# Attention and feed-forward on one core: the first two batches share seven products on half of w_in's columns, attention runs in two TensorE visits per pair, and the first pair is normalised ahead of the branch

**Chip, cores, metric.** One core of one Trainium2 chip. The metric is device microseconds of a whole execution; lower is better. The kernel before takes 1549 us, and its executions agree within 0.5%.

## The reference

```python
batch, n_heads, seq, head_dim = (8, 12, 448, 64)
n_tokens, d_model, d_ff = (3584, 768, 2048)

def rmsnorm(x, g):
    return x / np.sqrt(np.mean(x * x, axis=-1, keepdims=True) + 1e-06) * g
q_n, k_n = rmsnorm(q, g_q), rmsnorm(k, g_k)
scores = q_n @ k_n.transpose(0, 1, 3, 2) / np.sqrt(64)
attn = np.exp(scores - np.max(scores, axis=-1, keepdims=True))
attn = attn / (np.sum(attn, axis=-1, keepdims=True) + 1e-09)
x = heads_joined(attn @ v)                 # 3584 x 768
h = x @ w_in
out = (h * (1.0 / (1.0 + np.exp(-h)))) @ w_out
```

The arithmetic is fp32. The work is 48 pairs of heads (n = 0 to 47, six to a batch), then a second layer that only multiplies. The weights arrive in 64-bit words: ScalarE *opens* a piece of them, then VectorE and GpSimd *round* it to fp32.

## The kernel before

Both feed-forward layers use seven products of quarter matrices in place of eight (Strassen-Winograd); `sum_x` and `sum_w_in` form, on VectorE, the sums of quarters that these need. `seven` builds each product in one of two PSUM banks named mm, in the order 1 2 6 5 7 3 4; ScalarE empties products 1 and 5, VectorE the others. Each emptying is called its *eviction* here.

```python
def bank(n):
    return ps.tile([P, BANK], F32, name="mm", bufs=2)[:, 0:n]
...
    def product(name):
        t = bank(n)
        for i, s in enumerate(steps):
            nc.tensor.matmul(t, left(name, s), right(name, s), start=i == 0, ...)
            yield n
        return t
    nc.scalar.copy(p1, (yield from product("1")))
    plus((yield from product("2")), p1, done[1, 1])        # plus: a VectorE add
    plus((yield from product("6")), p1, u2)
    nc.scalar.copy(p5, (yield from product("5")))
    plus((yield from product("7")), u2, u3)
    ...                                                    # two adds on GpSimd
    plus((yield from product("3")), u2, done[1, 2])
    plus((yield from product("4")), u3, done[2, 1])
```

This is a generator. The loop over the pairs calls `fill()` to put some of its matmuls (*filler*) between parts of the attention. If a filler ends with a product's last matmul, that product's eviction is issued only when the next filler resumes the generator.

```python
def divide(n):
    t = ps.tile([P, S], F32, name="tr")      # one bank, also used by transpose()
    for h in range(2):
        nc.tensor.matmul(t[...], ones[0:R, :], es[:, h, :], start=True, stop=True)
    nc.vector.reciprocal(out=r, in_=t)
    nc.vector.tensor_tensor(out=xT(*pairs[n]), in0=xU, in1=r, op=ALU.mult)
...
for n, (b, hp) in enumerate(pairs):
    load(n + 2)
    scores(0);              fill()           # half of the scores
    if n > 0: divide(n - 1)                  # sums of e (ones), reciprocal, multiply
    ...
    weigh(n, 0); scores(1); add_up(0)
    ...                                      # batch 1: round w_in
    fill()
    transpose(n + 1, "q")
    weigh(n, 1); unload(n); add_up(1)
    ...
    fill()
    transpose(n + 1, "k"); normalise(n + 2)
    ...
    fill()
```

Batch 0 has no filler. In batches 1 to 3 the filler is `whole(0)`, batch 0's first layer by plain products (96 matmuls of 448 columns), then batch 1 alone by seven products of 224 columns. The pairs n = 24 to 35 carry the seven products of batches 2 and 3, and so on.

## Time and profile before

| | before |
|---|---|
| median of 4 runs | 1549.01 us (1548.05 to 1550.51) |
| span of the profiled run | 1543.8 us |
| mean granted TensorE clock | 0.991 |

### The profile page before, as it was taken

Reading aid. Unit: us, or ns where it says so; the run is one execution under the profiler, and the core shown is the slowest. Engines: PE = TensorE matmul, PEld = TensorE weight load, DVE = VectorE, ACT = ScalarE, POOL = GpSimd, SP = SyncE. Lnnn points to the kernel's source line nnn. Section 1 sums busy time; section 2 is a strip of 40 time slices with the busy share of each in tenths; the row PEclk is TensorE's granted clock in tenths of the full one; section 3 lists DMA queues with packets and bytes.
Section 4 is the critical chain, followed back from the end, with each engine's and each line's share of the span. In section 5 each row is a group of like instructions: output and inputs, shape, how many; then the busy total and the mean of one; then the engine's idle time right before and its main releaser. Section 6 shows DMA issues by size and latency. Waiting matters only on the chain. (4 is left out here: it accounts for less than half of the span.)

```text
span 1543.8 us, 14413 instructions
## 1 busy us (share of the span) xinstructions
PE 1464.2 (95%) x5216; PEld 743.5 (48%) x5216; DVE 759.0 (49%) x970; ACT 525.3 (34%) x744; POOL 408.7 (26%) x300
## 2 busy tenths in 40 slices
PE   5789999899899999999999989999999999999998
PEld 2234444555444444344444344445555555555554
DVE  4988876655765555665555575662121112121221
ACT  4558865555544544544444423420000000000000
POOL 4555533333333323332333223330000000000000
PEclk9999999999899999999999999999999999999999
DMA  6344221121211211311131064442222222222220
GB/s 194 96 128 144 72 78 55 60 61 60 72 60 48 85 59 42 103 60 60 42 102 42 27 212 131 155 149 76 75 75 75 75 75 75 75 75 86 75 85 23
DMA packets 87924, 128.96 MB, mean 84 GB/s; under 512 B 5924, under 2 KB 70948, under 8 KB 87844
## 3 DMA queue, kind: packets, MB, share of 16 engines
q1 hardware_dynamic: 87520, 127.95, 26.5%
q8 instruction: 43, 0.70, 0.2%
q14 instruction: 37, 0.30, 0.1%
q10 hardware_dynamic: 324, 0.00, 0.0%
HBM read 87.56 MB, written 40.37 MB: 83 GB/s over the span
## 5 line engine op out<-in xcount | busy, mean ns | idle before, releaser
L434 PE MATMUL mm<-x,W 128*128 128x448 f32 (+1 forms) x768 | 283.4, 507 | 14.7 <-DVE stage L408 13.1
L335 POOL TENSOR_TENSOR rms<-rms,minus_half 112x16 f32<-112x16 f32 x48 | 141.0, 2937 | 408.4 <-DVE rms L332 394.9
L368 ACT ACTIVATE work<-sc 112x896 f32<-112x896 f32 x192 | 166.1, 914 | 203.3 <-PE sc L365 203.0
L434 PE MATMUL mm<-sums_x,W 128*128 128x448 f32 (+1 forms) x576 | 210.9, 500 | 14.7 <-DVE parts L408 9.3
L434 PEld LDWEIGHTS mm<-x,W 128*128 128x128 f32 x768 | 141.1, 192 | 148.6 <-issue 122.8
L446 POOL TENSOR_TENSOR parts<-parts 128x448 f32<-128x448 f32 (+2 forms) x46 | 49.2, 1069 | 582.1 <-DVE parts L408 581.8
L434 PE MATMUL mm<-W,work 128*128 128x384 f32 x588 | 197.6, 486 | 0.0
L365 PE MATMUL sc<-work 64*112 64x448 f32 x768 | 175.4, 577 | 17.8 <-DVE work L358 17.8
L399 DVE RECIPROCAL work<-tr 128x448 f32<-128x448 f32 x48 | 141.8, 2953 | 88.7 <-PE tr L398 88.7
L408 DVE TENSOR_TENSOR stage<-mm,parts 128x448 f32<-128x448 f32 (+2 forms) x121 | 67.7, 562 | 237.5 <-PE mm L434 101.2
L408 DVE TENSOR_TENSOR parts<-mm,parts 128x448 f32<-128x448 f32 (+2 forms) x92 | 51.6, 561 | 265.7 <-PE mm L434 256.5
L388 DVE TENSOR_TENSOR work<-work 112x896 f32<-112x896 f32 x144 | 169.0, 1174 | 12.1 <-ACT work L368 5.5
L377 PE MATMUL av<-work,rows 112*64 112x448 f32 x768 | 165.3, 552 | 3.6 <-ACT work L368 3.6
L434 PEld LDWEIGHTS mm<-sums_x,W 128*128 128x128 f32 x576 | 104.5, 190 | 105.6 <-issue 79.5
L434 PEld LDWEIGHTS mm<-W,work 128*128 128x128 f32 x588 | 111.7, 190 | 77.9
L365 PEld LDWEIGHTS sc<-work 64*112 64x112 f32 x768 | 62.4, 176 | 115.7 <-issue 63.8
L441 ACT COPY parts<-mm 128x448 f32<-128x448 f32 (+2 forms) x46 | 21.8, 474 | 268.9 <-PE mm L434 268.9
L434 PE MATMUL mm<-W,x 128*128 128x384 f32 x336 | 112.9, 486 | 0.0
L340 POOL TENSOR_TENSOR work<-rows,rms 112x512 f32<-112x512 f32 x96 | 100.6, 1069 | 3.8
L444 ACT COPY parts<-mm 128x448 f32<-128x448 f32 (+2 forms) x46 | 22.1, 481 | 221.9 <-PE mm L434 221.9
L377 PEld LDWEIGHTS av<-work,rows 112*64 112x64 f32 x768 | 50.6, 138 | 82.3 <-issue 53.5
L434 PEld LDWEIGHTS mm<-W,x 128*128 128x128 f32 x336 | 63.8, 190 | 44.5
(66 smaller groups left out, 1437.4 us busy)
## 6 DMA issues: line engine op xcount, KB each, us to landing
hidden<-stage SPq DMA_DIRECT2D x48, 448.0 KB, 2.5
work<-hidden SPq DMA_DIRECT2D x7, 2048.0 KB, 9.0
x<-hidden SPq DMA_DIRECT2D x7, 2048.0 KB, 9.0
W<-in_moe_w_in_dram SPq DMA_DIRECT2D x24, 512.0 KB, 4.1
rows<-in_moe_w_out_dram SPq DMA_DIRECT2D x32, 384.0 KB, 3.1
rows<-in_q_dram SPq DMA_DIRECT2D x48, 224.0 KB, 3.6
rows<-in_k_dram SPq DMA_DIRECT2D x48, 224.0 KB, 3.8
rows<-in_v_dram SPq DMA_DIRECT2D x48, 224.0 KB, 3.6
```

Source lines behind the costliest of these rows:

```text
L335: nc.gpsimd.tensor_tensor(out=flat, in0=flat, in1=minus_half[0:R].to_broadcast([R, 4 * J]), op=ALU.pow)
L340: nc.gpsimd.tensor_tensor(out=normal[name].rearrange("p j h d -> p h j d"), in0=st[name], in1=factor.to_broadcast([R, 2, J, D]), op=ALU.mult,)
L365: nc.tensor.matmul(banks[:, h, 0:S], kT[rows, ts(j, R)], qT[rows, :], start=True, stop=True)
L368: nc.scalar.activation(e[j], banks[:, :, 0:S], AF.Exp)
L377: nc.tensor.matmul(st["av"][ds(h * D, D), :], st["v"][:, h, j, :], e[j][:, h, :], start=(j == 0), stop=(j == J - 1),)
L388: nc.vector.tensor_tensor(out=es, in0=e[0] if j == 1 else es, in1=e[j], op=ALU.add)
L399: nc.vector.reciprocal(out=r, in_=t)
L408: nc.vector.tensor_tensor(out=out, in0=a, in1=b, op=ALU.add)
L434: nc.tensor.matmul(t, left(name, s), right(name, s), start=i == 0, stop=i == len(steps) - 1)
L441: nc.scalar.copy(p1, (yield from product("1")))
L444: nc.scalar.copy(p5, (yield from product("5")))
L446: nc.gpsimd.tensor_tensor(out=u2, in0=u2, in1=p5, op=ALU.add)
```

## The change

The intent: no more 224-column products (batches 0 and 1 take plain products for the first half of w_in's columns and share seven full-width products for the second), one change of TensorE's form fewer per pair, and an earlier start. Cut to its core:

```diff
-        if name == "q":
-            nc.scalar.copy(features[name], t)
+        dst = features[name][n % 2]                    # qT and kT are doubled
+        if name == "q":
+            nc.scalar.copy(dst, t)
+        elif n < 2 * z.NPAIR:
+            nc.scalar.activation(dst, t, AF.Copy, scale=gains)
         else:
-            nc.vector.tensor_scalar_mul(out=features[name], in0=t, scalar1=gains)
+            nc.vector.tensor_scalar_mul(out=dst, in0=t, scalar1=gains)
...
     def first_two():
-        yield from whole(0)
+        yield from whole(1, early)                     # first 8 of 16 column blocks
         for c in range(HW):
-            sum_x([1], c)
-        yield from halves_in([1])
+            sum_x([0, 1], c)
+        yield from halves_in([0, 1], late)
...
+    def weights_in(n, point):                          # when w_in is rounded
+        if n < NPAIR:
+            count = point == 3
+        else:
+            count = n < 5 * NPAIR // 2 and (point % 2 or n < NPAIR + 3 and point == 0)
+        ...
-    for n, (b, hp) in enumerate(pairs):
-        (the loop shown above)
+    for n in range(last + 2):
+        b, hp = pairs[n] if n <= last else (z.B, 0)
+        if n <= last:
+            scores(n, 0)
+        if n > 0:
+            weigh(n - 1, 1)
+            unload(n - 1)
+            divide(n - 1)
+        load(n + 2)
+        ...                                            # begin a group of filler
+        weights_in(n, 0)
+        fill()
+        weights_in(n, 1)
+        transpose(n + 1, "q")
+        scores(n, 1)
+        weigh(n, 0)
+        add_up(0)
+        transpose(n + 1, "k")
+        add_up(1)
+        weights_in(n, 2)
+        ...                                            # at a group's end: finish(), sum_x
+        fill()
+        weights_in(n, 3)
+        normalise(n + 2)
```

Besides, `normalise` of pair 0 stands ahead of the branch (by the size of the gains the program picks one of two versions of itself), with VectorE in place of GpSimd for its multiply; the last two stores are halved; and the scratch for raw weights is smaller for the later half of w_in.

## The prediction

> **What bounds the kernel now.** I read the page first, then the groups by form, the chain of waits in order of time, and TensorE's timeline. n counts the 48 pairs of heads (six per batch), so n = 6 opens batch 1 and n = 24 batch 4.
>
> ```profile
> PE 1464.2 (95%) x5216; PEld 743.5 (48%) x5216; DVE 759.0 (49%) x970; ACT 525.3 (34%) x744; POOL 408.7 (26%) x300
> ...
> PE   5789999899899999999999989999999999999998
> ```
>
> TensorE is the bound in all but the first 100 us. A faster helper engine buys nothing; only TensorE's columns, its changes of form and its idle time count.
>
> ```profile
> L434 PE MATMUL mm<-sums_x,W 128*128 128x448 f32 x432 | 178.5, 548 | 13.0 <-DVE parts L408 9.3 <-ACT parts L441 2.8 <-DVE stage L408 0.9
> ...
> L388 DVE TENSOR_TENSOR work<-work 112x896 f32<-112x896 f32 x144 | 169.0, 1174 | 12.1 <-ACT work L368 5.5
> ...
> L399 DVE RECIPROCAL work<-tr 128x448 f32<-128x448 f32 x48 | 141.8, 2953 | 88.7 <-PE tr L398 88.7
> ...
> L434 PE MATMUL mm<-x,W 128*128 128x224 f32 x192 | 46.9, 376 | 13.9 <-DVE stage L408 12.3 <-ACT stage L472 1.6
> ```
>
> The last line is the weak spot that the change aims at: batch 1 alone runs its seven products on 224 columns, and these wait for VectorE to empty the two PSUM banks.
>
> ```profile
> 790.92 3.02 PE mm L434 x8
> 793.95 1.69 PE sc L365 x8
> 795.64 2.45 PE mm L434 x6
> 798.09 0.90 PE tr L398 x4
> 798.99 1.50 PE av L377 x8
> 800.50 1.69 PE sc L365 x8
> 802.19 3.20 PE mm L434 x8
> ```
>
> In this chain a matmul is two records. Eight mm records after transposes take 3.02 us, so a matmul of 448 columns takes 0.755; after scores the same eight take 3.20. One pair of steady state (n = 25 to 34) starts every 20.1 us with 15 such matmuls (11.3), so the pair's own attention work and changes of form cost 8.75.
>
> **What the Trainium skill says.** "TensorEngine Tiling (Array Packing)", Key Properties: changing the tiling mode drains TensorE. The trace agrees and prices it: 0.18 us (3.20 against 3.02). "TensorE: Matmul & The Clock Gate", section on the 16 sub-arrays: VectorE and ScalarE work strictly in order. The trace agrees:
>
> ```profile
> 519.91 2.96 DVE L399 RECIPROCAL work<-tr 128x448 f32<-128x448 f32 x1 [6.39 <-PE tr L398]
> 521.30 1.76 PE L365 MATMUL sc<-work 64*112 64x448 f32 x8
> ...
> 522.90 0.62 DVE L400 TENSOR_TENSOR x<-work 128x448 f32<-128x448 f32 x1
> 522.99 3.27 PE L434 MATMUL mm<-x,W 128*128 128x448 f32 x8
> ...
> 533.17 0.62 DVE L408 TENSOR_TENSOR stage<-mm,parts 128x448 f32<-128x448 f32 x1
> ...
> 533.84 1.02 PE L434 MATMUL mm<-x,W 128*128 128x448 f32 x2 [0.43 <-DVE stage L408]
> ```
>
> Here the eviction at 533.17 stood behind the reductions of the normalisation, and TensorE, with both banks full, lost 0.43 us. The same page, Part 1, says that about 3.4 us of idleness halve the clock; the trace agrees (scores took 2.70 us in place of 1.76 after 3.51 us idle at 53.93).
>
> **The change part by part.**
>
> *Shared seven products.* Before: 96 matmuls of 448 and 168 of 224 columns. After: 96 and 84 of 448. The columns are equal (80,640). In the timeline six records of 224 columns step by 1.23 us, 0.41 a matmul, so 168 took 69; 84 x 0.755 is 63.4. That saves about 5. From 255 to 408 us the timeline also lists idle times of 1.3 to 2.0 us, eleven of them, about 18 us in sum: they go, because a product of 448 columns lasts longer than its eviction. Gain some 23 us.
>
> *Two visits.* Per pair one change of form of seven goes: 42 pairs with filler x 0.15 = 6 us. I take 8.6 in place of 8.75.
>
> What it moves matters more. Before, the sums (ones) were followed by 3.2 us of weighing and scores, under which the reciprocal ran; then came filler. After, the build's order on TensorE is scores, weigh, ones, filler at once. VectorE's order is reciprocal, multiply, then evictions. From the filler's start: reciprocal at 0.2, end 3.2, multiply to 3.75, the first eviction done at 4.4. If a product ended just before this filler (its eviction is issued only with the next filler), the second product wants its bank at 0.18 + 3 x 0.755 = 2.45: 1.95 us lost. If it ends one matmul in, 3.2: 1.2 lost; two in, 0.45. Products 1 and 5 are emptied by ScalarE and lose nothing. In the second filler VectorE first scales kT (0.68, from batch 2 on) and does two sums of e (2.2 together), so evictions end at 3.6: 1.36, 0.6 or 0 lost.
>
> The build lists the filler sizes (8, 8, 7, 8, 8, 7 ... matmuls, 168 in 22 fillers). Going through them with the product order 1 2 6 5 7 3 4: first fillers lose 0.45 + 0.45 + 3 x 1.2 + 2 x 1.95 = 8.4, second ones 3 x 0.6 + 3 x 1.36 = 5.9; 14.3 us per group of two batches, 28.6 for n = 24 to 47. For n = 12 to 22 the fillers are exactly six, two whole products, so the second is always deferred: 4 x 1.95 + 4 x 1.36 = 13.2.
>
> *One burst.* At n = 16 VectorE does all twelve sums of x (12 x 0.62 = 7.5 us) and a sum_w_in (3.8) ahead of the eviction of product 2; product 5 wants that bank at 11.3 us after the filler's start and gets it at 19.5: 8.2 lost.
>
> *Head.* The first transposes were at 15.13, after GpSimd's multiply; with VectorE multiplying and no wait for the branch I get 12.6. But in batch 0 there is no filler, and the loop through the single buffer of normalised rows closes more slowly: from one transposition of q, transposes, scores and weigh 4.4, kT on ScalarE 0.55, raw weights opened 1.2, squares 1.15, reduction 0.75, pow 2.9, multiply 1.05, some waits 0.3: 12.3 us per pair, against 12.0 measured (41.79 to 53.93). So n = 6 starts near 90.7 as before, and the head's gain is eaten.
>
> *Tail.* Two last stores halved: 0.7.
>
> Sum by stage (start of scores to start of scores):
> - n = 0 to 5: 0.
> - n = 6 to 11: before 90.67 to 193.62 = 103.0. After 48 x 0.755 + 6 x 8.6 + 2 = 89.8. Gain 13.2.
> - n = 12 to 23: before to 412.79 = 219.2. After 132 x 0.755 + 12 x 8.6 = 202.9, + 13.2 + 8.2 + 1.5 = 225.8. Loss 6.6.
> - n = 24 to the end of the first layer (1031.7): before 618.9. After 504 x 0.755 + 24 x 8.6 = 586.9, + 28.6, + 11.3 for two group ends without filler, + 7.3 for the wait on w_out's first rows, + 9.3 for the four 2.33 us waits that stay = 643.4. Loss 24.5.
> - Second layer, 506 us of matmuls: unchanged.
>
> Loss 17. The new stalls (50 us) are my softest term: each assumes that the eviction comes at its latest. I count three quarters of them, which leaves a loss of 5: 1554.
>
> **The rivals.**
> 1. *The stalls hardly come*, because the bank is free earlier than I think. Then the loss turns into 1548.7 + 17 - 50 - 0.7 = 1515, faster by a bit over 2%. For it: TensorE waited only 15 us for VectorE on 448-column products in the kernel before, and the author's filler sizes look tuned. Against it: the reciprocal's 2.95 us are fixed and now stand at the head of a filler.
> 2. *The batch-0 loop goes cold.* TensorE idles over 3 us per pair there; if each visit runs at half clock, the pair takes some 2 us more, 12 us in all: about 1566.
> 3. *ScalarE becomes the bound for n = 6 to 8.* Exp 3.7, three openings 3.6, copies and squares 2.7, one and a half SiLU with table loads 4.7: about 14.7 us in a pair of 15. If it slips, 3 to 6 us more: about 1559.
>
> **Range and chances.** From rival 1 halfway (1530) to all stalls and rival 2 (1578): 1526 to 1578. Faster by over 2% needs under 1518, nearly the whole of rival 1: 0.12. Slower needs over 1580: 0.09.
>
> **What would show it.** Right: the groups by form show no 128x224 matmuls; idle time ahead of L452's matmuls put down to VectorE rises from about 15 to 35 to 50 us; the reciprocal stands before it in the timeline; pairs of n = 24 to 34 start every 21 us rather than 20.1 to 20.8; n = 6 to 11 shorter by over 10 us; scores of n = 6 near 90 us. Wrong: pairs of n = 24 to 34 at 20 us, or batch 0 under 11 us a pair, which makes the change faster than I say.

## More of the kernel before

The prediction shows the page, groups, chain and timeline. One view more serves as the ruler for all that follows: busy time by stretch of the kernel before. The five stretches run from the start of the scores of one pair to that of another (n = 0, 6, 12, 24, 36), the last one to the end of the first layer. The columns are start:end, length, then busy us (records) of TensorE, its weight loads, VectorE, ScalarE and GpSimd, then the granted TensorE clock (1.00 is full speed; I call it cold where it is clearly less), the DMA share and GB/s.

```profile
18.58:90.67 72.09, 56.96 (x261) 20.81 (x261) 61.35 (x68) 40.52 (x62) 38.22 (x23) 0.95 0.36 99
90.67:193.62 102.95, 99.20 (x386) 41.52 (x386) 86.60 (x110) 78.06 (x109) 57.53 (x36) 1.00 0.38 117
193.62:412.79 219.17, 201.10 (x935) 114.96 (x935) 136.66 (x179) 121.45 (x163) 70.50 (x53) 0.98 0.21 65
412.79:651.12 238.33, 234.24 (x864) 101.65 (x865) 136.95 (x161) 108.45 (x143) 81.25 (x52) 0.99 0.19 63
651.12:1031.73 380.61, 364.94 (x1197) 165.53 (x1197) 230.10 (x321) 157.83 (x234) 128.26 (x97) 0.99 0.29 94
```

Length minus the first busy column is TensorE's idle time. From n = 24 to 35 it is 238.33 - 234.24 = 4.1 us in twelve pairs: there is little left to win there, and much that a new order can lose.

## The result, and the profile after

| | before | after |
|---|---|---|
| median of 4 runs | 1549.01 us | 1602.62 us (1601.32 to 1603.70) |
| span of the profiled run | 1543.8 us | 1601.9 us |
| mean granted TensorE clock | 0.991 | 0.982 |

The ratio of after to before is 1.0345, 95% interval 1.0327 to 1.0363: **slower by 3.4%**, outside the predicted range. Ratios here and below are the mean time of one kernel's fast runs over that of the other's of the same rounds, so not quite the ratio of the medians that I quote. All kernels below gave correct results.

The page of the kernel after, its TensorE lines:

```profile
PE 1475.1 (92%) x5048; PEld 717.5 (45%) x5048; DVE 758.3 (47%) x940; ACT 524.9 (33%) x738; POOL 404.6 (25%) x290
...
PE   4778999799899999989999989999999999999998
```

168 records fewer, yet TensorE is busy 11 us longer, and idle longer too. Where, the same five stretches of the kernel after tell (from n = 0 again):

```profile
17.24:105.62 88.38, 63.67 (x252) 23.73 (x252) 58.59 (x64) 42.97 (x66) 37.45 (x23) 0.86 0.29 84
105.62:204.17 98.55, 89.97 (x360) 37.85 (x361) 79.09 (x91) 76.90 (x108) 54.69 (x33) 0.98 0.38 115
204.17:436.37 232.20, 209.89 (x792) 89.28 (x793) 144.35 (x169) 116.73 (x152) 76.06 (x48) 0.97 0.21 64
436.37:693.02 256.65, 237.94 (x864) 102.66 (x865) 136.56 (x161) 109.88 (x144) 79.26 (x52) 0.98 0.19 61
693.02:1090.63 397.61, 365.78 (x1204) 164.96 (x1205) 231.90 (x323) 159.89 (x236) 126.13 (x97) 0.99 0.27 88
```

| stretch | change of length | of which idle | of which busy | predicted change |
|---|---|---|---|---|
| start to n = 6 | +15.0 (start -1.3, pairs +16.3) | +9.6 | +6.7 | 0 |
| n = 6 to 11 | -4.4 | +4.8 | -9.2 | -13.2 |
| n = 12 to 23 | +13.0 | +4.2 | +8.8 | +6.6 |
| n = 24 to end of first layer | +35.3 | +30.8 | +4.5 | +24.5 |
| second layer and tail | -0.8 | | | -0.7 |
| sum | +58.1 | | | +17.2 |

The busy columns of n = 6 to 23 must be read together, since the change moves some 9 us of matmuls from the first of these stretches to the second. The prediction's last step then took a quarter off the new waits and came to +5. The trace of the kernel before is of a run of 1545.57 us, some 3 us faster than the four of the table, so the traces differ by 58 us and the medians by 54.

The groups by form answer to the prediction's test: no 128x224 form is left, and the idle time ahead of the full-width products has grown to 55.7 us, most of it put down to VectorE. In the kernel before it was 13.9 us for those and 15.5 for the 224-column form.

```profile
L452 PE MATMUL mm<-x,W 128*128 128x448 f32 x672 | 272.6, 549 | 20.8 <-DVE stage L426 17.3 <-ACT parts L462 2.5 <-DVE parts L426 1.0
L452 PE MATMUL mm<-sums_x,W 128*128 128x448 f32 x504 | 212.0, 560 | 34.9 <-DVE stage L426 16.0 <-DVE parts L426 15.8 <-ACT parts L459 3.0
```

**The stall, seen.** Timeline of the kernel after, TensorE and VectorE, in pair 32:

```profile
614.07 2.52 PE L452 MATMUL mm<-sums_x,W 128*128 128x448 f32 x6
614.21 2.96 DVE L417 RECIPROCAL work<-tr 128x448 f32<-128x448 f32 x1 [4.30 <-PE tr L416]
617.27 0.62 DVE L418 TENSOR_TENSOR x<-work 128x448 f32<-128x448 f32 x1
617.81 1.15 DVE L426 TENSOR_TENSOR stage<-mm,parts 128x448 f32<-128x448 f32 x2
618.48 4.97 PE L452 MATMUL mm<-x,W 128*128 128x448 f32 x8 [1.90 <-DVE stage L426]
...
623.29 0.55 PE L368 MATMUL tr<-ident,qn 112*128 112x112 f32 x4
```

The filler starts at 614.07 with one product (six records). Its second needs the bank of the product before, whose eviction was deferred to this filler and so stands in VectorE's queue behind the reciprocal and the multiply. TensorE waits 1.90 us; the prediction said 1.95. But then eight records take 4.97 us, where eight at full clock take 3.27 in this view (522.99 in the prediction's lines). The busy view of three small windows of the kernel after (the filler, the wait, the 2 us after it) shows why:

```profile
614.10:616.60 2.50, 2.49 (x8) 1.02 (x6) 2.39 (x1) 1.24 (x1) 1.78 (x2) 1.00 0.37 92
616.60:618.48 1.88, 0.00 (x0) 0.00 (x0) 1.77 (x4) 0.02 (x1) 0.00 (x0) 1.00 0.00 0
618.48:620.50 2.02, 2.02 (x3) 0.97 (x4) 1.48 (x2) 1.77 (x2) 0.00 (x0) 0.56 0.12 46
```

The granted clock is 1.00 up to the wait and 0.56 right after it. From 614.07 to the next transposes, 623.29, are 9.22 us, where seven matmuls at 0.755 take 5.29: this wait cost 3.9 us in all.

**The burst, seen.** Timeline of the kernel after at n = 16:

```profile
288.52 2.43 PE L452 MATMUL mm<-sums_x,W 128*128 128x448 f32 x6
...
291.06 2.70 DVE L423 TENSOR_TENSOR W<-W 128x768 f32<-128x768 f32 x3
...
297.46 0.62 DVE L426 TENSOR_TENSOR stage<-mm,parts 128x448 f32<-128x448 f32 x1
298.13 2.61 PE L452 MATMUL mm<-sums_x,W 128*128 128x448 f32 x3 [7.18 <-DVE stage L426]
```

The sums of x and of w_in pass ahead of the eviction: 7.18 us lost; the prediction said 8.2. Afterwards three records take 2.61 us, against some 1.4 at full clock (two take 1.02 at 533.84 in the prediction's lines, one more adds 0.38).

**Batch 0, seen.** Timeline of the kernel after in the time of pair 2 (VectorE, GpSimd and TensorE, other lines left out):

```profile
51.84 2.96 DVE L417 RECIPROCAL work<-tr 128x448 f32<-128x448 f32 x1 [1.11 <-PE tr L416]
53.78 1.04 POOL L293 TENSOR_TENSOR qn<-rows,rms 112x512 f32<-112x512 f32 x1
...
54.94 0.57 PE L368 MATMUL tr<-ident,qn 112*128 112x112 f32 x4 [3.15 <-POOL qn L293]
55.45 3.29 PE L383 MATMUL sc<-work 64*112 64x448 f32 x8
```

TensorE is idle for 3.15 us before the transposes of q, and the scores after them take 3.29 us in place of 1.76: half clock. From one start of scores to the next a pair takes 13.8 to 16.6 us, most often 14.14, where the kernel before took 12.0. Two things end at nearly the same moment before 54.94: GpSimd's rows of q (53.78 + 1.04 = 54.82) and the reciprocal (51.84 + 2.96 = 54.80), which reads the one bank tr that the transposes also write. The profile names only the later of the two.

### The profile page after: what moved, and what is told of

The parts are those of the page before. It is cut to its first block, busy times and chain, and to the rows that moved or that the text cites. A ratio compares the mean times of both kernels' runs of the same rounds, so it can differ in the third digit from the quotient of the medians.

```text
span 1601.9 us, 13991 instructions
## 1 busy us (share of the span) xinstructions
PE 1475.1 (92%) x5048; PEld 717.5 (45%) x5048; DVE 758.3 (47%) x940; ACT 524.9 (33%) x738; POOL 404.6 (25%) x290
## 5 line engine op out<-in xcount | busy, mean ns | idle before, releaser
L452 PE MATMUL mm<-x,W 128*128 128x448 f32 x672 | 272.6, 549 | 20.8 <-DVE stage L426 17.3
L452 PE MATMUL mm<-sums_x,W 128*128 128x448 f32 x504 | 212.0, 560 | 34.9 <-DVE stage L426 16.0
L464 POOL TENSOR_TENSOR parts<-parts 128x448 f32<-128x448 f32 (+1 forms) x42 | 49.1, 1169 | 646.6 <-DVE parts L426 646.3
L452 PEld LDWEIGHTS mm<-x,W 128*128 128x128 f32 x672 | 123.8, 191 | 156.1 <-issue 115.4
L426 DVE TENSOR_TENSOR parts<-mm,parts 128x448 f32<-128x448 f32 (+1 forms) x84 | 50.4, 599 | 223.2 <-PE mm L452 223.2
L452 PEld LDWEIGHTS mm<-sums_x,W 128*128 128x128 f32 x504 | 93.8, 194 | 137.8 <-issue 82.1
L426 DVE TENSOR_TENSOR stage<-mm,parts 128x448 f32<-128x448 f32 (+1 forms) x109 | 65.4, 606 | 163.8 <-PE mm L452 87.1
L459 ACT COPY parts<-mm 128x448 f32<-128x448 f32 (+1 forms) x42 | 21.4, 509 | 277.7 <-PE mm L452 277.7
L462 ACT COPY parts<-mm 128x448 f32<-128x448 f32 (+1 forms) x42 | 21.6, 515 | 273.3 <-PE mm L452 273.3
L375 DVE TENSOR_SCALAR work<-tr,gains 128x448 f32<-128x448 f32 x36 | 24.6, 683 | 138.1 <-PE tr L368 137.8
L552 ACT ACTIVATE stage<-stage 128x896 f32<-128x896 f32 x56 | 52.3, 948 | 112.5 <-DVE stage L426 89.1
```

The lines of the kernel that those rows point to most:

```text
L375: nc.vector.tensor_scalar_mul(out=dst, in0=t, scalar1=gains)
L426: nc.vector.tensor_tensor(out=out, in0=a, in1=b, op=ALU.add)
L464: nc.gpsimd.tensor_tensor(out=u2, in0=u2, in1=p5, op=ALU.add)
L552: nc.scalar.activation(rows[i], rows[i], AF.Silu)
```

## The experiments

My theory after the result: (a) the reciprocal at the head of a filler, with deferred evictions behind it, makes the new waits; (b) batch 0 is slow by idle time and then by clock; (c) the shared products are good in themselves. The rivals: that the waits are not of the deferral but of the new order as such; that batch 0 is only as slow as its loop of buffers; that the waits come in any order of this kernel.

The times in one table; before was run beside each (medians 1548.73 to 1549.68 us):

| run | edit | median us | ratio to before, 95% |
|---|---|---|---|
| after | | 1602.62 | 1.0345 (1.0327 to 1.0363) |
| e1 | after, ones ahead of the scores | 1572.88 | 1.0153 (1.0136 to 1.0170) |
| e2 | after, evictions at once | 1561.95 | 1.0088 (1.0071 to 1.0105) |
| e3 | after, clock kept warm in batch 0 | 1596.84 | 1.0310 (1.0293 to 1.0328) |
| e4 | before, shared products only | 1540.73 | 0.9950 (0.9933 to 0.9967) |
| e5 | after, normalise ahead of rounding | 1605.46 (its four fast runs) | 1.0356 (1.0329 to 1.0384) |
| e6 | after, two rounds of w_in a pair | 1599.96 | 1.0321 (1.0294 to 1.0348) |
| e7 | before, ones next to the filler | 1658.57 | 1.0705 (1.0673 to 1.0737) |
| e8 | after, e1 + e2 + e5 + e6 | 1544.79 | 0.9967 (0.9941 to 0.9992) |
| e9 | after, own bank for the ones | 1604.95 | 1.0364 (1.0343 to 1.0385) |
| e10 | after, e9 + e5 | 1595.75 | 1.0297 (1.0271 to 1.0323) |
| e11 | after, e8 + e9 | 1534.50 | 0.9909 (0.9889 to 0.9928) |
| e12 | before, evictions at once | 1541.59 | 0.9952 (0.9932 to 0.9973) |

### e1_ones_first: is it the reciprocal at the head of the filler?

```diff
-        if n <= last:
-            scores(n, 0)
         if n > 0:
             weigh(n - 1, 1)
             unload(n - 1)
             divide(n - 1)
+        if n <= last:
+            scores(n, 0)
```

> The changed kernel with one edit: in the first visit of a pair the weighing of the pair before, its sums (ones) and its division stand ahead of the scores, so that 1.7 us of scores lie over the reciprocal before the filler begins. Theory (reciprocal at the head of the filler holds back the evictions): in the first fillers the waits of 1.87 to 1.90 us shrink to about 0.2 and those of 1.12 and 0.37 go, some 21 us in all and some 5 us of cold clock after them: about 1577 us in place of 1602.6. Rival (the banks are full for another reason, or batch 0 alone made the loss): under 5 us of gain, and the 1.9 us waits stay.

Measured 1572.88 us: 30 us of the 54 come back. From n = 24 to 35 the length falls from 256.65 to 242.73 us: idle time from 18.7 to 10.6, and busy time from 237.9 to 232.1, with the granted clock at 1.00. So putting 1.7 us of scores between the reciprocal and the filler removes 8.1 of the 18.7 us of idle time, and it removes cold clock with it. Batch 0 got 4 us worse (92.40 us), as there the scores now start later.

### e2_at_once: is it the deferred eviction?

```diff
                 nc.tensor.matmul(t, left(name, s), right(name, s), ...)
-                yield n
+                if i < len(steps) - 1:
+                    yield n
             return t
...
         plus((yield from product("2")), p1, done[1, 1])
+        yield n
         plus((yield from product("6")), p1, u2)
+        yield n                     # and so on after each eviction
```

> The changed kernel with one edit: the eviction of a product is issued in the filler in which its last matmul stands, not with the next filler (the filler's generator yields after the eviction). Theory (a third of the evictions, and with six matmuls a filler every second one, are deferred behind the reciprocal or behind kT and the sums of e): the 7.18 us wait at n = 16 falls to about 0.5, the waits of 1.87 to 1.90 and of 1.23 us in fillers that begin with a new product go, some 30 us: about 1572 us. Products that end one or two matmuls into a filler still wait (1.12, 0.37, 0.48 us). Rival (only the reciprocal matters, however the evictions are issued): the sum of VectorE waits stays above 40 us and the time within 5 us of 1602.

The plain products of `whole` are edited in the same way. Measured 1561.95 us: 41 of the 54 us. n = 12 to 23, where every filler ends with a product, goes from 232.20 to 213.12 us, which is less than the 219.17 of the kernel before; n = 24 to 35 from 256.65 to 245.77. The timeline of this kernel at the burst:

```profile
285.87 2.43 PE L452 MATMUL mm<-sums_x,W 128*128 128x448 f32 x6
288.55 2.52 PE L452 MATMUL mm<-sums_x,W 128*128 128x448 f32 x6 [0.24 <-DVE stage L426]
293.83 1.76 PE L383 MATMUL sc<-work 64*112 64x448 f32 x8 [2.76 <-DVE work L375]
```

The wait of 7.18 us is down to 0.24; VectorE's burst is as long as it was, and 2.76 us of it show up as a wait for kT. e1 and e2 attack the same waits from two sides, so their gains do not add. What is left over n = 24 to 35 tells them apart. The waits of 1.90 us are gone in both kernels: they need both the reciprocal and a deferred eviction behind it. In e1 three waits of 1.24 us stay, in second fillers, where no reciprocal stands ahead; in e2 two of 1.12 us stay, of products that end one matmul into a filler, whose evictions are not deferred.

### e3_warm: is batch 0 slow by clock?

```diff
         weights_in(n, 0)
+        if 0 < n < NPAIR:
+            t = bank(P)
+            for _ in range(12):
+                nc.tensor.matmul(t, ident, ident, start=True, stop=True)
         fill()
```

> The changed kernel with one edit: in batch 0 (pairs 1 to 5) twelve matmuls of the identity with itself, 128 columns, read by nobody, fill the idle time after the ones. Theory (the pair takes 14.4 us there because TensorE idles over 3 us in each pair and then runs its scores at half clock, 3.3 us in place of 1.7): scores in 1.76 us, 12.3 to 12.7 us a pair, 8 to 10 us less in all: about 1593 us. Rival (the loop through the normalised rows takes 14.4 us whatever the clock): the same time or a little more, since the idle time is only filled.

Timeline of this kernel:

```profile
61.82 2.94 PE L710 MATMUL mm<-ident 128*128 128x128 f32 x24
65.04 0.57 PE L368 MATMUL tr<-ident,qn 112*128 112x112 f32 x4 [0.28 <-POOL qn L293]
65.54 1.76 PE L383 MATMUL sc<-work 64*112 64x448 f32 x8
```

With 2.94 us of useless matmuls in the gap, all scores from 40.55 us on take 1.76 us, a pair takes 12.49 us, and the scores of n = 6 start at 95.20 in place of 105.62. The prediction's 12.3 us a pair was right for a warm clock. The traced span fell by 9.7 us, the median by 5.8.

### e4_shared_only: what are the shared products worth alone?

```diff
     def first_two():
-        yield from whole(0)
+        yield from whole(1, range(z.NF // 2))
         for c in range(HW):
-            sum_x([1], c)
-        yield from halves_in([1])
+            sum_x([0, 1], c)
+        yield from halves_in([0, 1], blocks=range(HF // 2, HF))
...
             if b == 1 and hp == 0:
-                begin(first_two(), ...)
+                begin(whole(0, range(z.NF // 2)), ...)
+            elif b == 2 and hp == 0:
+                begin(first_two(), ...)
```

> The kernel before with the first part of the change alone: batches 0 and 1 share seven products on the second half of w_in's columns, with the four short fillers of the kernel before and nothing else of the change. Theory of the prediction: the 128x224 products cost 5 us in matmuls and 18 us in waits, so about 1549 - 23 = 1526 us. Rival (the shared products bring their own burst of sums of x and w_in, or the matmuls were never the cost): within 8 us of 1549.

A miss: 1540.73 us, 8 us faster, where I had said 23. Two reasons. First, the matmuls themselves save nothing. In the timeline of the kernel before, a long run of 224-column records:

```profile
354.43 2.06 PE L434 MATMUL mm<-sums_x,W 128*128 128x224 f32 x10
356.32 0.55 PE L354 MATMUL tr<-ident,work 112*128 112x112 f32 x4
```

Ten records in 356.32 - 354.43 = 1.89 us are 0.378 us per matmul (two records), exactly half of 0.755. I had taken 0.41 from runs of six, which hold a change of form. The Trainium skill would have set me right: "FP8 and Floating Point Precision", TensorE Precision Notes, counts four passes for true fp32; at the 2.4 GHz of "TensorE: Matmul & The Clock Gate", Part 1, that is an estimate of 4 x 224 / 2.4 = 373 ns and 747 ns for 448 columns. The trace agrees, with 378 and 755. Second, waits of another kind came. Over n = 12 to 23 the waits for evictions fall from 15.5 us to 2.3 and idle time from 18.1 to 7.5, while busy time (more of the matmuls lie there now) goes from 201.1 to 207.4. But n = 6 to 11 has 8.2 us of idle time where it had 3.8: in pair 11 the filler of batch 0 has run out, and the first scores of n = 12, at 189.75, wait 4.40 us for kT, which VectorE scales only after a rounding of w_in. The twelve sums of x, now in one place, delay other scores by 1.52 us (279.93).

### e5_norm_first and e9_own_bank, then e10_bank_norm: what holds batch 0?

e5 asks whether GpSimd's rounding of w_in delays its rows of q; e9 whether the reciprocal delays the transposes through the bank tr; e10 does both.

```diff
         fill()
+        if n < NPAIR:
+            normalise(n + 2)
         weights_in(n, 3)
-        normalise(n + 2)
+        if n >= NPAIR:
+            normalise(n + 2)
```

```diff
     def divide(n):
-        t = ps.tile([P, S], F32, name="tr")
+        t = bank(S) if n < z.NPAIR - 1 else ps.tile([P, S], F32, name="tr")
```

> The changed kernel with one edit: in batch 0 the normalisation of the pair after next is issued ahead of the rounding of w_in, so the two opening activations (1.2 us a pair) no longer stand between the transposes and the squares. Theory (the loop through the one buffer of normalised rows, 12.5 us with a warm clock, leaves TensorE idle for over 3 us, and that makes the clock cold): the loop falls to about 11.3 us, the idle time to about 2 us, the scores stay at 1.76 us; n = 6 starts near 90 us in place of 105.6: about 1588 us. Rival (the loop is set by something other than ScalarE's order, such as the rounding on VectorE and GpSimd, which now stands behind the normalisation): the pairs stay at 14 us and the time within 4 us of 1602.

> The changed kernel with one edit: in batch 0 the ones write a bank of mm, which no filler uses yet, and not the one bank tr that the transposes of q need next. Theory: in batch 0 two loops of almost the same length stand side by side (the reciprocal that holds the bank tr ends within 0.1 us of GpSimd's multiply that delivers the rows of q, so the profile names only one); taking away one of them alone changes little: within 4 us of 1602.6. Rival (the reciprocal alone sets the loop): some 12 us less, 1590.

> The changed kernel with both edits for batch 0: ones in their own bank, and the normalisation ahead of the rounding of w_in (which alone gave nothing, 1606). Theory of the two loops: with both gone the idle time before the transposes of q falls from 3.15 us to 1 to 2, the clock stays warm, a pair takes 10.5 to 11.5 us in place of 14.4, n = 6 starts near 85 to 88 us in place of 105.6: about 1584 us. Rival (batch 0 is bound by something else, such as ScalarE or the loads): within 5 us of 1602.

e5 missed: no gain, its four fast runs took 1603.80 to 1606.10 us. (Its profiled run fell in a slow state of 3083.06 us, so its trace is not used.) e9 gave 1604.95, no gain, which by then was expected. e10 gave 1595.75, and its scores of n = 6 start at 95.0 in place of 105.6. So two loops of equal length run side by side, and cutting either alone shows nothing. A third kernel, e8 (below), has e5's edit and lets one see the bank at work. Its timeline in batch 0:

```profile
49.53 2.96 DVE L417 RECIPROCAL work<-tr 128x448 f32<-128x448 f32 x1 [0.71 <-PE tr L416]
50.47 1.04 POOL L293 TENSOR_TENSOR qn<-rows,rms 112x512 f32<-112x512 f32 x1
...
52.64 0.98 PE L368 MATMUL tr<-ident,qn 112*128 112x112 f32 x4 [3.15 <-POOL kn L293]
```

The rows of q are ready at 51.51 and the transposes still start at 52.64, just after the reciprocal ends (52.49). The line puts the wait down to the rows of k, which the transposes of q do not read. In e10, with both edits, the wait is 2.07 us and pairs take 11.4 us at full clock, 13.1 to 13.3 cold. I had expected 1584: even 2 us of idle time let the clock fall in some pairs.

### e6_two_a_pair: is n = 6 to 8 held by ScalarE?

```diff
-            count = n < 5 * NPAIR // 2 and (point % 2 or n < NPAIR + 3 and point == 0)
+            count = n < 5 * NPAIR // 2 and (point % 2 or n < NPAIR + 1 and point == 0)
```

> The changed kernel with one edit: from n = 7 on two pieces of w_in a pair are rounded in place of three for n = 7 and 8. Theory (for n = 6 to 8 ScalarE, with three openings and SiLU with its table loads, is late with the copy of qT, and the transposes of k wait 1.7 to 2.1 us for it): these waits fall from 5.8 us to about 2 and n = 6 to 11 takes some 4 us less: about 1598 us. Rival (ScalarE is not the bound, the copies wait for the table loads of the SiLU alone): the same time.

n = 6 to 11 falls from 98.55 to 91.83 us, near the 89.8 of the prediction: the three waits of the transposes of k for ScalarE's copy of qT (1.66 + 1.98 + 2.14 = 5.8 us) fall to 1.66 + 0.22 us. The median fell by 2.7 us only: from n = 24 on, where nothing was changed, TensorE was busy 4.1 us longer (239.59 and 368.27 us), at granted clocks of 0.97 and 0.98 in place of 0.98 and 0.99. Which waits cool the clock seems to shift with the timing.

### e7_late_divide: does the same order hurt the kernel before?

```diff
         fill()
+        weigh(n, 0)
+        scores(1)
         if n > 0:
             divide(n - 1)
         ...
-        weigh(n, 0)
-        scores(1)
         add_up(0)
```

> The kernel BEFORE with one edit in the other direction: the ones and the division of the pair before are issued after the weighing and the scores, so that the reciprocal stands at the head of a filler, as in the changed kernel; nothing else changes. Theory (a reciprocal at the head of a filler holds the evictions back): fillers of four matmuls that begin with a new product lose up to 1.9 us, a third of them less those that ScalarE empties, about 0.4 us a pair in mean, 10 to 20 us in all: about 1564 us, with waits of 1.2 to 1.9 us put down to VectorE right after the ones. Rival: within 4 us of 1549.

The direction was right and the size far off: +109 us. Here another victim appears, as the timeline of this kernel shows:

```profile
262.32 1.77 PE L467 MATMUL mm<-x,W 128*128 128x448 f32 x4
...
265.54 0.57 PE L354 MATMUL tr<-ident,work 112*128 112x112 f32 x4 [1.45 <-DVE work L399]
```

This kernel has four fillers a pair, and here the one after the ones lasts 1.77 us, less than a reciprocal, while the transposes that follow want the bank tr. In batch 0, with no filler at all, these waits sum to 15.8 us; over n = 12 to 23 the waits for evictions are 27.6 us. It confirms that the reciprocal's place matters, not how large the effect in the kernel after should be.

### e8_combo1 and e11_combo2: the repairs together

e8 is the kernel after with the edits of e2, e5, e6, and of e1 from n = 6 on. e11 adds the bank of e9.

> The changed kernel with four repairs together: evictions issued at once, ones ahead of the scores from n = 6 on, the normalisation ahead of the rounding in batch 0, two pieces a pair. If the causes are separate, from 1562 (evictions at once) some 8 to 10 us go with the reciprocal's cover, some 14 with batch 0 and some 4 with the pieces: about 1535 us, so faster than the kernel before (1549) by about 1%. If they share one cause, no better than 1555.

> All repairs of the changed kernel together: evictions at once, ones ahead of the scores from n = 6 on, two pieces a pair, and in batch 0 the normalisation first and the ones in their own bank. From 1544.8 (without the bank) some 16 us go with batch 0: about 1529 us, the fastest so far, 1.3% under the kernel before. If batch 0 is bound otherwise: 1545.

e8: 1544.79 us. e11: 1534.50 us, 68 us under the kernel after, 0.9% faster than the kernel before, and the fastest of all. Both fell short of what I expected (by 10 and 5.5 us). By stretch, e11 has 78.74 us for n = 0 to 5, still 6.7 more than before; 95.16, 211.36, 238.74 and 379.65 for the rest: 7.8, 7.8, -0.4 and 1.0 less. So the two visits, repaired, win nothing from n = 24 to 35. Pairs without waits are shorter by 0.25 us there (19.85 us with 15 matmuls, so 8.52 for the attention in place of 8.77), but the waits at the ends of groups take it back.

### e12_before_at_once: a control

e2's edit on the kernel before.

> Control: the kernel BEFORE with the evictions issued at once and nothing else. Theory (late issue of an eviction costs time only where a long VectorE instruction heads the filler; in the kernel before the weighing and the scores cover the reciprocal): within 4 us of 1549. Rival (late issue costs by itself, in any order): 10 us or more faster.

A miss: 7 us faster, where I had expected no change. n = 12 to 23, with its short products, gains 10.9 us (waits for evictions 13.9 to 5.4); n = 24 to 35 gains 1.6, which is the "no change" of the expectation for full-width products; and the last stretch loses 10.3. Of these 7.45 are idle time: in the last group, which has no filler, four waits of 2.3 us become four of 4.2. I did not test why. So the deferred eviction cost the kernel before something too, where products are short.

## Why the prediction was wrong

I predicted 1554 us (+5) and got +54 in the medians, +58 in the traces. Setting the prediction's terms beside the measured stretches, split into TensorE's idle and busy time:

| stretch | idle, predicted | idle, measured | busy, predicted | busy, measured |
|---|---|---|---|---|
| n = 6 to 11 | 2.0 | 8.6 | 87.8 | 90.0 |
| n = 12 to 23 | 22.9 | 22.3 | 202.9 | 209.9 |
| n = 24 to end of first layer | 56.5 | 50.5 | 586.9 | 603.7 |

So from n = 6 on, the waits of the full working came to 81.4 us in both columns, by luck in part: of the 50 us of new stalls 43 came (17.7, 12.5 and 12.8 us of filler waits for n = 12 to 23, 24 to 35 and 36 to 47), and 6.6 us that were not counted came in n = 6 to 11. The busy time was 26 us short. With the 15 us of batch 0 and the 12 of the discount these make up the 53 us between forecast and trace.

- **The first failing step: "n = 0 to 5: 0", which put the cold clock of batch 0 among the rivals.** 15 us. The 12.3 us a pair are what a warm clock gives (12.49 in e3); with idle times of 3.15 us in each pair the clock fell, and the pairs took 13.8 to 16.6. Rival 2 was the truth, with 15 us for its 12. The working also knew only one of the two loops that close there (the rows, not the bank; e5, e9, e10).
- **The second: busy time priced from undisturbed pairs and set against measured lengths.** 26 us. The same prices (0.755 a matmul, 0.378 for one of 224 columns, 8.75 a pair), put on the kernel before, give 98.6, 194.9 and 590.5 us for the three stretches, where its trace has 99.2, 201.1 and 599.2. So 15.5 of the 26 us are missing there too: a gain that the forecast counted and that was never to be had, not a cost of the change. The other 10 are new, and go with the waits, some 24 more than before, which the working counted at their own length. Cold clock follows them: one minus the granted clock, times the length, gives an estimate of 18 us for the kernel after and 11 for the kernel before, rough as the clocks have two digits. And ahead of each wait the view books the modelled end of the last matmul as busy (six records are listed with 2.52 us and step by 2.27). The runs do not part the two. e1 and e11 support that the waits are behind it: with the waits gone, busy time of the same matmuls from n = 24 to 35 fell by 5.8 and 5.6 us.
- **The third: "I count three quarters of them".** 12 us taken off, where at most 7 failed to come (less, if the modelled ends are counted to the waits). Single stalls came in nearly full: 1.87 to 1.90, 1.12 and 0.37 us in the first fillers for 1.95, 1.2 and 0.45; 1.24 and 0.48 in the second for 1.36 and 0.6; 7.18 for the burst's 8.2. The discount had no line of the profile behind it.
- **n = 6 to 11.** The waits were 8.6 us, not 2. This was rival 3, seen, sized at 3 to 6 us and left out of the sum (e6).
- **Shared products: a gain of 23.** Worth 8 alone (e4). The 0.41 us for a 224-column matmul was a misreading, and the waits that go are partly replaced by waits for kT. The "eleven" idle times are ten (17.0 us), and one of them, 1.78 us at 408.18, is for the bank tr; the waits for evictions were 15.5 us.
- **Two slips that did not matter.** The waits for VectorE on 448-column products in the kernel before were 11.1 us, not 15, and rival 1's 1515 takes off the tail's 0.7 us twice.
- **Right:** the mechanism of the stalls and its arithmetic (e1, e2), the saving of a form change (8.6 us predicted, 8.52 in pairs without waits), the tail's 0.7 us. The head was half right: the first transposes came at 13.84, not 12.6, as the product of the gains on VectorE waited for a load of g_k until 8.34 and held the squares' reductions behind it.
- **The group ends** I set at 11.3 us for two. In the trace of the kernel after they cost 7.9 us each, cold clock included (a pair of 14.28 us without filler, less 8.52, and 2.14 ahead of the next transposes of q).

What stays open: which of the waits near 2 us cool the clock and which don't, and how much of the busy time that the prices miss, in either kernel, is cold clock.

## What to carry to other kernels

When a long instruction moves on an engine that works in order, list what queues behind it and which PSUM bank each of these frees; here the waits of single fillers came within 0.12 us of the count, and 43 of 50 us in sum. Then price each TensorE wait of about 2 us at up to twice its length, for the clock that it may cost (3.9 us in all for 1.90 at 618.48). Put your prices on the kernel before as well: what they miss there (15.5 us here) is no gain of the change. And where one wait is cured without any gain, look for a second loop of the same length: the profile names only the releaser that came last.

## What the Trainium skill lacked or had wrong

- "TensorE: Matmul & The Clock Gate", Part 1: it gives about 3.4 us of idleness as what halves the clock. Here a wait of 1.90 us between full fillers was enough (granted clock 1.00 before, 0.56 after, at 618.48). Others did nothing (1.87 us at 371.12, 2.22 us at 875.47: the matmuls after them ran at full clock); why, no run here shows.
- The same page, section on LDWEIGHTS: P / 1.2, which is 107 ns for 128 columns. The fp32 loads of 128x128 took 190 to 194 ns on the mean.
- "TensorEngine Tiling (Array Packing)", Key Properties: a change of mode drains TensorE, but no price is given. Here 0.18 us for one change, and 0.25 us a pair for a visit saved.
- No page that I found prices VectorE's reciprocal: 2.957 us for 128x448 fp32, against 0.62 for a sum of the same size reading PSUM.
- No page that I found tells of a whole execution like one run of e5: 3083 us, its 128x448 matmuls at 1026 ns on the mean in place of 549, with a granted clock of 1.000 in the records.
